# Gated linear attention and two MLPs: the first chunk's loads walked by groups of tokens

## The chip, the cores and the metric

The kernel runs on one core of one Trainium2 chip, in one launch. The metric is the time on the device in microseconds (us). The median of three runs before the change is 977.85 us (976.86 to 978.01).

A core has TensorE (matmuls; PE, with PEld for its weight loads), VectorE (DVE), ScalarE (ACT), GpSimd (POOL) and SyncE (SP), each with its own queue of instructions that it works through in order, and 16 DMA engines that carry what SyncE's and ScalarE's queues issue. SBUF is the on-chip memory of 128 partitions, PSUM the smaller one that TensorE writes.

## The reference

Four sequences (B) of 768 tokens (S) with 8 heads (H) of 48 features (D) go through a gated linear attention; its output, 3072 tokens of 384 features, goes through two MLPs of 2048 hidden units.

```
f = 1 / (1 + exp(-f_logit))
for t in range(S):
    state = f[:, :, t, :, None] * state + einsum('bhd,bhe->bhde', k[:, :, t], v[:, :, t])
    y[:, :, t] = einsum('bhd,bhde->bhe', q[:, :, t], state)
x = y with heads side by side, (B * S, H * D)
h = x @ w_in;   g = max(h, 0) + alpha * min(h, 0);  x = g @ w_out     # first MLP
h = x @ w_in2;  g = h - tanh(h);                    out = g @ w_out2  # second MLP
```

All is float32; the weights come as float64 and are decoded to float32 on the chip.

## The kernel before, in words

The 768 tokens are cut into 6 chunks of 128 (C). A step of the attention is one sequence and one chunk, 24 in all; steps 0 to 3 are the first chunk of the four sequences, and they are the ones with i < EARLY. A step has seven stages: f (transpose f_logit, make the gate, two scans up and down), k (transpose k and q, scale them to kd and qd), s0 and s1 (the scores sc = kd times qd, masked to a; kr and ks, kd turned back), y0 and y1 (the output y from a and v, split into x, the MLP's input), m (the new state from ks and v). A unit of the MLP is one chunk of all four sequences, 512 tokens, and one block of 128 hidden units: nine matmuls h (L451 to L453), the activation on ScalarE and VectorE, nine matmuls acc (L511). Its first needs x of all four steps of the first chunk and the first decoded block of weights.

Every load is issued by load_step (f, k, q and later v), load_v (v of the first chunk: va at L183, two vb at L185) or load_w (weights, L197 to L216), nearly all on SyncE's queue. For steps 0 to 3, each of f, k and q comes in two loads (L167), one for even heads and one for odd ones, 96 KB each. In such a load a partition holds four consecutive tokens (j) of one pair of heads, one row of 4 x 48 floats, 768 bytes; there are 32 groups of tokens (t) and four pairs (p), 128 partitions. From step 4 on, a load (L175) has one token in a partition, in rows of 192 bytes, and 192 KB. Of the 24 loads of L167, the three for odd heads of step 0 are issued by ScalarE, the other 21 by SyncE.

turned() puts features on the partitions. For steps 0 to 3 it makes eight matmuls (two halves of heads, four j) against the identity, so that a column of the PSUM tile is a partition of the loaded tile. The view that it returns orders these columns by pair, group and j again, and ScalarE (L266) and VectorE (L292, L294) read it through that view and write plain tiles. Nothing after that depends on how the load placed the rows.

The order of the stages and loads up to the first unit of the MLP is the list PROLOGUE, written by hand: loads of steps 0, 1, v of 0, step 2, the first weights, v of 1, step 3, v of 2, two more blocks of weights, with v of 3 and the loads of step 4 behind the stages of step 0. A planner that estimates times when the kernel is built then lays down each engine's order of instructions; on the chip each engine keeps that order. Behind the prologue, the list work places attention steps, loads and decoding of weights between the MLP's units by due times. Three buffers hold f, k and q by turns (NV), and three hold raw weights (NR), so later loads are issued as buffers come free.

Of the kernel before, what the change touches and what calls it, by code (L numbers as in the profile page):

```python
# [20 lines left out]
C = 128  # L21
NC = S // C
UT = B * C
NP = H // 2
# [46 lines left out]
def tile_main(tc, q, k, v, f_logit, w1_in, w1_out, alpha, w2_in, w2_out, out, flag):  # L71
    nc = tc.nc
    with ExitStack() as ctx:
# [37 lines left out]
        for b in range(2):  # L111
            t = const.tile([128, NP, 2, HW], F32, name=f"blocks{b}")
# [11 lines left out]
        def set_idle(t, nm):  # L124
            for a, b in ((4 * D, PAD), (PAD + 4 * D, H * HW)):
                nc.vector.memset(t[:, a:b], 30.0 if nm == "f" else 0.0)

        padded = {}
        for nm in ("f", "k", "q"):
            padded[nm] = []  # L130
            for j in range(NV):
                t = const.tile([128, H * HW], F32, name=f"{nm}{j}")
# [15 lines left out]
        def load_step(i):  # L148
            c, b = divmod(i, B)
            t0 = c * C  # L150
            s = {}
            for nm, a in (("f", f_logit), ("k", k), ("q", q), ("v", v)):
                if nm == "v" and c == 0:
                    continue
                if nm == "v":
                    t = s[nm] = ld.tile([128, H, D], F32, tag=nm, name=nm, bufs=NV)
                else:
                    if i == NV:
                        t = tp.tile([128, H * HW], F32, **{"f": dict(tag="g"), "k": dict(tag="g"), "q": dict(tag="neg", bufs=1)}[nm], name=nm)
                        set_idle(t, nm)  # L160
                    else:
                        t = padded[nm][i % NV]
                    if i < EARLY:

                        s[nm] = t[:, 0:2 * PAD].rearrange("p (h x) -> p h x", h=2)
                        for h in range(2):
                            (nc.scalar if i == 0 and h else nc.sync).dma_start(  # L167
                                out=s[nm][:, h, 0:4 * D],
                                in_=a[b, h::2, t0:t0 + C, :].rearrange("p (t j) d -> p t (j d)", j=4),
                            )  # L170
                        continue

                    s[nm] = t.rearrange("p (h x) -> p h x", h=H)
                    t = s[nm][:, :, 0:D]
                nc.sync.dma_start(out=t, in_=a[b, :, t0:t0 + C, :].rearrange("h t d -> t h d"))  # L175
            steps[i] = s
# [65 lines left out]
        def turned(i, nm, palloc):  # L242

            a = steps[i][nm]
            if i >= EARLY:
                t = palloc([128, NP, C], nm + "t")
                for p in range(NP):
                    nc.tensor.transpose(t[:, p], a[:, 2 * p:2 * p + 2, :].rearrange("t h d -> t (h d)"), ident)  # L248
                return t
            t = palloc([128, 4, 128], nm + "t")  # L250
            for j in range(4):
                for h in range(2):
                    nc.tensor.matmul(
                        out=t[HW * h:HW * h + HW, j], lhsT=a[:, h, j * D:j * D + HW], rhs=ident, start=True, stop=True
                    )
            return t.rearrange("p j (h t) -> p h t j", h=NP)

        def like(i, a):

# [2 lines left out]
        def attn_f(i, palloc):  # L262
            s = steps[i]
            gv = spread(gate[:, 0:NP * SEG])
            ft = turned(i, "f", palloc)
            nc.scalar.activation(out=like(i, gv), in_=ft, func=ACTF.Exp, scale=-1.0)  # L266
            if i < 2 * B:
                nc.scalar.activation(out=gv, in_=gv, func=ACTF.Identity, bias=ones[:, 0:1])  # L268
            else:
                nc.vector.tensor_scalar(out=gv, in0=gv, scalar1=1.0, scalar2=None, op0=ALU.add)  # L270
            up = at.tile([128, NP * SEG], F32, tag="up", name="up")
            nc.vector.tensor_tensor_scan(  # L272
                out=up, data0=gate[:, 0:NP * SEG], data1=reset, initial=0.0, op0=ALU.mult, op1=ALU.add
            )
            ends = up[:, C:NP * SEG:SEG]
            inv = carry[:, SEG:NP * SEG + 1:SEG]
            nc.vector.reciprocal(out=inv, in_=ends)
            nc.vector.tensor_tensor(out=worst, in0=worst, in1=ends, op=ALU.max)
            down = at.tile([128, NP * SEG + 1], F32, tag="down", name="down")
            nc.vector.tensor_tensor_scan(  # L280
                out=down[:, NP * SEG:0:-1], data0=gate[:, NP * SEG:0:-1], data1=carry[:, NP * SEG:0:-1],
                initial=0.0, op0=ALU.mult, op1=ALU.add,
            )
            ends = at.tile([128, NP], F32, tag="inv", name="inv", bufs=3)
            nc.vector.tensor_copy(out=ends, in_=inv)
            s.update(up=up, down=down, inv=ends)

        def attn_k(i, palloc):
            s = steps[i]
            kt, qt = turned(i, "k", palloc), turned(i, "q", palloc)  # L290
            kd = at.tile([128, NP, C], F32, tag="kd", name="kd")
            nc.vector.tensor_tensor(out=like(i, kd), in0=kt, in1=like(i, spread(s["up"])), op=ALU.mult)  # L292
            qd = at.tile([128, NP, C], F32, tag="qd", name="qd")
            nc.vector.tensor_tensor(  # L294
                out=like(i, qd), in0=qt, in1=like(i, spread(s["down"][:, 1:NP * SEG + 1])), op=ALU.mult
            )
            s.update(kd=kd, qd=qd, a=at.tile([128, 2, NP, C], F32, tag="a", name="a"))
# [282 lines left out]
        for ev in PROLOGUE:  # L580
            if ev[0] == "c":
                convert(0, ev[1])
            elif ev[0] == "w":
                load(0, ev[1])
            elif ev[0] == "l":
                load_step(ev[1])
            elif ev[0] == "v":
                load_v(ev[1])
            elif ev[0] == "a":
                nc.sync.dma_start(out=alpha_raw, in_=alpha.rearrange("(c p) -> c p", p=128))  # L590
            else:
                stage(*ev, wide)
# [10 lines left out]
        for i in range(B, NC * B):  # L603
            c, b = divmod(i, B)

            if c < 3:
                t0, order = (0.7, 24.7)[c - 1] + 1.85 * b, tight_order
            else:
                t0, order = (c - 1) * FC + 3 * b + (2.5 if c == 3 else 0.5), wide_order
            for st, t in order:  # L610
                if ("f", i) not in PROLOGUE or st != "f":
                    put(t0 + t, stage, st, i)
            if i >= B + NV:
                put(t0 - NV * (1.85 if c < 3 else 3) + 0.8, load_step, i)
        first = sum(ev[0] == "c" for ev in PROLOGUE)
        when = {2: 0, 3: 1.2, 4: 2.0, 5: 3.2, 6: 4.2, 7: 5.4}
        for n in range(2 * NG):
            t = when.get(n, 7.5 + 1.5 * (n - NG)) if n >= first else -0.3
# [10 lines left out]
        for n, (g, half) in enumerate(halves):  # L629
            t = max(last + 6 + 1.5 * n, last + 2 * g + 2 * half + 2.2)  # L630
# [173 lines left out]
```

## Time and profile before

| | us |
|---|---|
| median of three runs | 977.85 |
| the profiled execution | 977.85 |
| its span, first to last instruction | 975.8 |
| TensorE busy | 943.2 (97%) |
| VectorE busy | 560.9 (57%) |
| ScalarE busy | 408.4 (42%) |
| GpSimd busy | 9.6 (1%) |
| 62.68 MB by DMA, mean over the span | 64 GB/s |

The engines' shares are means over the span. A window gives the busy time of each engine in one stretch, TensorE's granted clock (1.00 is 2.4 GHz, 0.50 is 1.2), the mean share of time in which the 16 DMA engines had a packet under way (packets of several queues can overlap, so it can pass 1), and the bytes moved. A wait is put down to what ended last before the waiting instruction started.

### The profile page before, as it was taken

The page shows a single profiled execution, that of the slowest core. Times are in us where ns is not written, and L with a number is a line of the kernel's source. Part 1 is how long each engine was busy: PE and PEld are TensorE (multiplying, and loading weights), DVE is VectorE, ACT ScalarE, POOL GpSimd, SP SyncE. Part 2 cuts the span into 40 slices and gives each one's busy share as a digit, 9 for nine tenths or more (in the row PEclk, how much of TensorE's full clock was granted, in tenths as well). Part 3 has the DMA queues.
Part 4 walks back from the last instruction along what each step waited for, and adds up shares of the span by engine and source line. Part 5 has one row for each costly group of instructions (what it writes and reads, how often), then busy time and mean ns, then how long its engine had stood idle before and what let it go on. Part 6 is the DMA issues. An engine that isn't in the chain of part 4 may idle for free.

```text
span 975.8 us, 13398 instructions
## 1 busy us (share of the span) xinstructions
PE 943.2 (97%) x5299; PEld 779.7 (80%) x5299; DVE 560.9 (57%) x926; ACT 408.4 (42%) x721; POOL 9.6 (1%) x24
## 2 busy tenths in 40 slices
PE   5598999999999999999999999999999999999997
PEld 5577787888888887888888888888888888888896
DVE  5589998566655565456444899953343433433432
ACT  3265556444444443444344665532232332322222
POOL 2000000000000000000000000000000000000000
PEclk9789999999999999999999999999999999999999
DMA  4897845042421232112022336330030110200201
GB/s 103 149 190 162 148 107 116 9 110 44 82 50 33 49 85 47 25 36 62 8 67 65 122 105 194 98 65 0 1 66 1 22 44 0 33 1 1 33 1 35
DMA packets 154277, 62.68 MB, mean 64 GB/s; under 512 B 123856, under 2 KB 141664, under 8 KB 154208
## 3 DMA queue, kind: packets, MB, share of 16 engines
q1 hardware_dynamic: 153812, 61.47, 28.4%
q8 instruction: 43, 0.70, 0.3%
q10 hardware_dynamic: 396, 0.29, 0.1%
q14 instruction: 26, 0.21, 0.1%
HBM read 49.55 MB, written 10.22 MB: 61 GB/s over the span
## 4 chain that ended last, share of the span: by engine, by line
PE 90%; DMA 4%; DVE 3%; SPq 2%; issue 0%; ACT 0%; ACTq 0%; DVEq 0%
PE acc L511 40%; PE h L451 13%; PE h L452 13%; PE h L453 13%; PE sc L319 2%; PE y L366 2%; PE y L342 2%; DMA k<-in_k_dram 2%; PE kt L248 1%; DMA raw<-in_moe_w_in_dram 1%; PE m L401 1%; PE qt L248 1%; PE ft L248 1%; SPq L167 1%; PE kr L305 1%; DMA f<-in_f_logit_dram 1%
## 5 line engine op out<-in xcount | busy, mean ns | idle before, releaser
L451 PE MATMUL h<-x,wih 128*128 128x512 f32 x576 | 228.6, 397 | 2.4 <-DMA x<-x 2.4
L452 PE MATMUL h<-x,wih 128*128 128x512 f32 x576 | 225.0, 391 | 0.0
L453 PE MATMUL h<-x,wil 128*128 128x512 f32 x576 | 225.0, 391 | 0.0
L511 PE MATMUL acc<-gh,wol 128*128 128x512 f32 x528 | 206.8, 393 | 1.8 <-DVE wol L233 1.8
L511 PE MATMUL acc<-gl,woh 128*128 128x512 f32 x528 | 207.6, 393 | 0.0
L511 PE MATMUL acc<-gh,woh 128*128 128x512 f32 x528 | 201.4, 396 | 0.9 <-ACT woh L232 0.9
L472 ACT CAST gh<-g 128x512 fp32r<-128x512 f32 x192 | 119.2, 621 | 139.4 <-DVE g L464 73.6
L473 DVE TENSOR_TENSOR gl<-g,gh 128x512 fp32r<-128x512 f32 x192 | 132.1, 688 | 76.5 <-ACT gh L472 67.9
L464 DVE TENSOR_TENSOR g<-h,g 128x512 f32<-128x512 f32 x96 | 66.2, 689 | 146.0 <-ACT g L463 146.0
L459 DVE SCALAR_TENSOR_TENSOR g<-neg,alpha_neg,g 128x512 f32<-128x512 f32 x96 | 72.0, 750 | 123.1 <-ACT neg L458 123.0
L463 ACT ACTIVATE g<-h 128x512 f32<-128x512 f32 x96 | 57.5, 599 | 174.8 <-PE h L453 174.8
L451 PEld LDWEIGHTS h<-x,wih 128*128 128x128 f32 x576 | 108.2, 188 | 24.6 <-DMA x<-x 2.8
L453 PEld LDWEIGHTS h<-x,wil 128*128 128x128 f32 x576 | 108.1, 188 | 23.2 <-DVE dec L65 0.2
L452 PEld LDWEIGHTS h<-x,wih 128*128 128x128 f32 x576 | 108.3, 188 | 20.9
L511 PEld LDWEIGHTS acc<-gh,wol 128*128 128x128 f32 x528 | 99.3, 188 | 22.6 <-DVE wol L233 1.9
L511 PEld LDWEIGHTS acc<-gh,woh 128*128 128x128 f32 x528 | 99.1, 189 | 22.9 <-ACT woh L232 1.5
L511 PEld LDWEIGHTS acc<-gl,woh 128*128 128x128 f32 x528 | 99.6, 189 | 20.4 <-DVE gl L473 0.4
L457 ACT ACTIVATE g<-h 128x512 f32<-128x512 f32 x96 | 57.5, 598 | 130.5 <-PE h L453 129.6
L458 ACT ACTIVATE neg<-h 128x512 f32<-128x512 f32 x96 | 56.9, 593 | 0.0
L272 DVE TENSOR_TENSOR_SCAN up<-gate,reset 128x516 f32<-128x516 f32 x24 | 29.5, 1231 | 10.5 <-ACT gate L268 9.9
L319 PEld LDWEIGHTS sc<-qd,kd 48*128 48x128 f32 x384 | 26.5, 193 | 9.0 <-issue 4.6
L319 PE MATMUL sc<-qd,kd 48*128 48x128 f32 x384 | 31.4, 291 | 1.2 <-DVE qd L294 1.2
(99 smaller groups left out, 805.8 us busy)
## 6 DMA issues: line engine op xcount, KB each, us to landing
raw<-in_moe_w_out_dram SPq DMA_DIRECT2D x16, 768.0 KB
raw<-in_moe_w_in_dram SPq DMA_DIRECT2D x8, 768.0 KB
raw<-in_moe_w_in_dram SPq DMA_DIRECT2D x16, 288.0 KB
x1d<-o SPq DMA_DIRECT2D x24, 192.0 KB
x1raw<-x1d SPq DMA_DIRECT2D x6, 768.0 KB
f<-in_f_logit_dram SPq DMA_DIRECT2D x20, 192.0 KB
k<-in_k_dram SPq DMA_DIRECT2D x20, 192.0 KB
q<-in_q_dram SPq DMA_DIRECT2D x20, 192.0 KB
```

What stands on the lines that cost most here:

```text
L319: nc.tensor.matmul(out=sc[h][:, p], lhsT=s["kd"][r, p], rhs=s["qd"][r, p], start=True, stop=True)
L451: nc.tensor.matmul(out=h, lhsT=a, rhs=xh[:, r], start=(r == 0), stop=False)
L452: nc.tensor.matmul(out=h, lhsT=a, rhs=xl[:, r], start=False, stop=False)
L453: nc.tensor.matmul(out=h, lhsT=b, rhs=xh[:, r], start=False, stop=(r == 2))
L457: nc.scalar.activation(out=g, in_=h, func=ACTF.Relu)
L458: nc.scalar.activation(out=neg, in_=h, func=ACTF.Relu, scale=-1.0)
L459: nc.vector.scalar_tensor_tensor(out=g, in0=neg, scalar=alpha_neg[:, fc:fc + 1], in1=g, op0=ALU.mult, op1=ALU.add)
L463: nc.scalar.activation(out=g, in_=h, func=ACTF.Tanh)
L464: nc.vector.tensor_tensor(out=g, in0=h, in1=g, op=ALU.subtract)
L472: nc.scalar.copy(out=gh, in_=g)
L473: nc.vector.tensor_tensor(out=gl, in0=g, in1=gh.bitcast(F32), op=ALU.subtract)
L511: nc.tensor.matmul(out=t, lhsT=a, rhs=b, start=first and i == 0, stop=final and i == 2)
```

## The change

The access pattern of the 24 loads at L167 names the 32 groups of tokens first and the four pairs of heads second; before, it was the other way round. The rows, their 768 bytes and their count stay. So partition 4t + p holds group t of pair p, where it was 32p + t. The view at L256 takes that back: in a block of 128 columns the pair is now the inner part.

```
                             (nc.scalar if i == 0 and h else nc.sync).dma_start(
                                 out=s[nm][:, h, 0:4 * D],
-                                in_=a[b, h::2, t0:t0 + C, :].rearrange("p (t j) d -> p t (j d)", j=4),
+                                in_=a[b, h::2, t0:t0 + C, :].rearrange("p (t j) d -> t p (j d)", j=4),
                             )
...
-            return t.rearrange("p j (h t) -> p h t j", h=NP)
+            return t.rearrange("p j (t h) -> p h t j", h=NP)
```

## Rows read from the trace of the kernel before

**Rows 1.** The page's part 1: busy us of each engine, its share, instructions.

```profile
PE 943.2 (97%) x5299; PEld 779.7 (80%) x5299; DVE 560.9 (57%) x926; ACT 408.4 (42%) x721; POOL 9.6 (1%) x24
```

**Rows 2.** Windows by stage: length, busy us (instructions) by engine, TensorE's clock, DMA share, GB/s.

```profile
5.80:12.00 6.20, 5.10 (x50) 4.11 (x50) 2.79 (x5) 1.32 (x2) 0.00 (x0) 1.00 0.27 92
...
28.00:30.00 2.00, 0.66 (x2) 0.29 (x2) 0.57 (x2) 0.00 (x0) 0.00 (x0) 0.50 0.29 67
...
42.00:44.00 2.00, 2.00 (x46) 2.00 (x46) 0.62 (x3) 1.83 (x3) 1.20 (x2) 1.00 0.98 334
...
52.00:54.00 2.00, 1.61 (x10) 0.99 (x9) 1.97 (x5) 1.07 (x2) 0.83 (x2) 0.50 1.34 178
...
59.00:87.00 28.00, 25.38 (x187) 20.36 (x185) 27.96 (x49) 18.11 (x33) 0.00 (x0) 1.00 0.96 182
...
87.00:975.80 888.80, 879.99 (x4650) 726.63 (x4650) 501.54 (x800) 370.88 (x654) 0.00 (x0) 1.00 0.24 56
```

**Rows 3.** TensorE's waits, first 100 us: waiter, releaser, total us, times, longest.

```profile
PE ft L253 <- DMA f<-in_f_logit_dram: 8.4, 4, 5.8
...
PE y L354 <- DMA va<-in_v_dram: 5.4, 1, 5.4
...
PE m L401 <- DMA va<-in_v_dram: 2.1, 1, 2.1
```

**Rows 4.** Order of time on TensorE: start us, duration us, instruction [idle before, releaser].

```profile
5.78 1.98 PE L253 MATMUL ft<-ident,f 128*64 128x128 f32 x16 [5.78 <-DMA f<-in_f_logit_dram]
...
21.71 1.16 PE L319 MATMUL sc<-qd,kd 48*128 48x128 f32 x16
...
29.18 0.66 PE L354 MATMUL y<-a,va 128*64 128x128 f32 x2 [5.35 <-DMA va<-in_v_dram]
...
42.50 1.06 PE L253 MATMUL kt<-ident,k 128*64 128x128 f32 x16
...
44.91 0.82 PE L358 MATMUL y<-a,vb 128*64 128x128 f32 x12
...
48.01 0.52 PE L248 MATMUL ft<-ident,f 128*128 128x128 f32 x3 [2.27 <-DMA f<-in_f_logit_dram]
...
59.04 0.48 PE L451 MATMUL h<-x,wih 128*128 128x512 f32 x1
```

**Rows 5.** Order of time on SyncE's queue, its issues: start us, duration us.

```profile
0.82 0.75 SPq L167 DMA_DIRECT2D f<-in_f_logit_dram  x1
...
40.34 0.80 SPq L175 DMA_DIRECT2D f<-in_f_logit_dram  x1
```

**Rows 6.** SyncE's issues by line: ns min/median/max, first and last start us.

```profile
L167 SPq DMA_DIRECT2D q<-in_q_dram x7: 528/530/1664, 2.3 to 30.2; - x7
...
L183 SPq DMA_DIRECT2D va<-in_v_dram x4: 401/720/1873, 11.3 to 38.2; - x4
...
L185 SPq DMA_DIRECT2D vb<-in_v_dram x8: 546/995/1622, 12.3 to 39.4; - x8
...
L209 SPq DMA_DIRECT2D raw<-in_moe_w_in_dram x4: 434/436/444, 20.1 to 37.2; - x4
```

**Rows 7.** Order of time on GpSimd (first row) and VectorE.

```profile
23.61 1.23 POOL L325 TENSOR_SCALAR_AFFINE_SELECT a<-a 128x512 f32<-128x512 f32 x2 [5.16 <-ACT a L324]
...
38.24 0.69 DVE L292 TENSOR_TENSOR kd<-kt,up 128x512 f32<-128x512 f32 x1
...
47.38 0.96 DVE L65 SCALAR_TENSOR_TENSOR dec<-raw,dec 128x768 int32<-128x768 int32 x1
...
50.90 0.96 DVE L233 TENSOR_TENSOR wil<-dec,wih 128x768 fp32r<-128x768 f32 x1 [2.09 <-ACT wih L232]
...
51.77 1.23 DVE L272 TENSOR_TENSOR_SCAN up<-gate,reset 128x516 f32<-128x516 f32 x1
```

**Rows 8.** ScalarE's reads of PSUM by line: ns min/median/max.

```profile
L266 ACT ACTIVATE gate<-ft x6: 597/600/615, 7.8 to 59.4; 128x512 f32<-128x512 f32 x6
...
L307 ACT COPY ks<-kr x4: 586/586/604, 14.0 to 49.1; 128x512 f32<-128x512 f32 x4
```

## The prediction

> **What bounds the kernel now.** I read the engines' totals first [rows 1], then the windows by stage [rows 2], then TensorE's waits [rows 3], and last the order of time on TensorE, SyncE, VectorE and GpSimd [rows 4 to 7]. Over the whole span TensorE is busy 97%. After 87 us it is busy 879.99 of 888.80 us, and from 59 to 87 VectorE is busy 27.96 of 28.00 us while TensorE has 25.38 [rows 2]. So from 59.04 us, where the first matmul of the first layer starts [rows 4], the kernel runs at the pace of its engines. What can be saved is before that: the prologue, in which the four steps of the first chunk are computed. There TensorE's longest waits end with a DMA: 8.4 us for f in four waits (5.8 of it the start), 5.4 for va, 2.1 for va again [rows 3], 2.3 for the f of step 4 [rows 4].
>
> The view by windows says why these loads are late. From 5.8 to 12 us almost nothing but the loads of L167 is under way, and the DMA engines are busy 0.27 of 16, that is 4.3 engines, at 92 GB/s; from 28 to 30 us it is the same, 0.29 at 67 GB/s [rows 2]. From 42 to 44 us, with other loads, the same engines move 334 GB/s at a share of 0.98. So a load of L167 seems to run on four engines, as many as its outer dimension has entries.
>
> By the Trainium skill, "DMA: Bandwidth & Descriptors", section "Why a DMA increments its semaphore by 16 and not by 1", a DMA runs on the largest number of engines up to 16 that divides the slowest dimension of both its sides. By that rule it was gcd(4, 128) = 4 and becomes 16, and the trace's 0.27 agrees with the first half; the second half no run has shown yet.
>
> **The change, part by part.** It adds and removes no instruction. Each of the 24 loads of L167 (21 on SyncE's queue, 3 on ScalarE's) keeps its 128 rows of 768 bytes and its 96 KB; the order in which they are walked changes, and with it which partition holds which token and pair. That is undone by another view of the same PSUM tile at L256, read by three instructions a step.
>
> *The transposed read.* ACT at L266 and VectorE at L292 and L294 now step 1 over pairs and 4 over groups instead of 32 and 1; the innermost step stays 128 elements. ACT reads the present strided view in 600 ns and a plain 128x512 tile in 586 [rows 8]. So a stride of 128 costs at most 0.014 us; for 12 reads in four steps I take 0, between -0.2 and +0.2.
>
> *The transfer.* If 16 engines work on a load, 92 GB/s becomes at most four times that, 368; nearest row 334. The floor is no gain, 92. I take about 330, as the rows are neither shorter nor fewer. The 24 loads are 2.36 MB: 25.6 us of four engines' time at 92 GB/s, 7.1 at 334.
>
> *SyncE's queue.* It issues f of step 4 at 40.34 us [rows 5], after 43 issues: 21 of L167, 12 of v, 9 of weights, one of alpha. The queue starts at 0.82 us [rows 5]. At the shortest duration of each line (0.53 for L167, alpha taken the same; va 0.40 and vb 0.55; weights 0.43 [rows 6]), with 0.05 between two, f of step 4 goes out at 0.8 + 11.7 + 6.0 + 3.9 + 2.1 = 24.5 us. The other 15.8 us are issues held back by earlier loads that have not landed (L167 up to 1.66 us, against 0.53 [rows 6]). With quick landings they go. I take 0.53 for the new form too, between 0.43 (16 partitions or more, L209) and 1.66, the longest of its own line; the short values are those of a queue that isn't backed up.
>
> *The path through compute*, step by step:
> 1. First matmul: 5.78 us [rows 4]. Step 0's two f loads are 196 KB, 2.1 us at 92 GB/s and 0.6 at 334. I take 1.35 us of the 1.5, as the loads of k start in between.
> 2. Step 1: TensorE's 2.1 us for va go [rows 3], ft of step 1 no longer waits, and the scans of step 0 are the bound until step 1's run. The scores of step 1, at 21.71 [rows 4], come 2.6 to 4.0 us earlier; I take 3.3.
> 3. Its masks on GpSimd end at 23.61 + 1.23 = 24.84 [rows 7], so 21.5 in future. TensorE now waits until 29.18 for va [rows 4]; with va there, it starts y of step 1 at 21.5, 7.7 us earlier.
> 4. From there to kt of step 2, TensorE has y (2 x 0.82), kt (1.06), ft of step 3 (16 matmuls of the same shape, 1.06) and m (taken at 0.7, below the 1.06 of wider ones) [rows 4]: 4.5 us, to 26.0. Now kd of step 2 starts at 38.24 [rows 7]; the difference of 12.2 holds f's waits and the half clock of 0.50 [rows 2], which followed TensorE's idle time. Behind the waits VectorE's scans are late next (step 2's end 3.3 us earlier than now, about 25.3), so I count on 12.1.
> 5. The stretch from there to y of step 2 (44.91 + 0.82 = 45.73 [rows 4]) is compute and moves as it is. Then TensorE waits 2.3 us for f of step 4, 7.6 us after its issue. Issued at 24.5 it lands at about 32.1, and TensorE comes to it at 33.6: the wait goes, with 1.5 us to spare. But the weights' decoding on VectorE ends at 48.34 (47.38 + 0.96) and its scan at 51.77 [rows 7] must follow the weights' split (wil, 0.96 [rows 7], and ScalarE's cast before it, taken the same): not before 50.3. So 1.5 of the 2.3 count.
>
> The sum is 12.1 + 1.5 = 13.6 us if all of that holds, 12.9 with 2.6 in step 2, and 11.4 if the wait for f of step 4 also stays in another guise. I take 12.8: the first matmul of the layer then starts at 46.2 instead of 59.04. Behind it nothing is added: the stretch bound by VectorE and the one bound by TensorE move as a whole, since loads there are issued as buffers come free and move along (DMA share 0.96 from 59 to 87, so hardly more could be had).
>
> The profiled execution took 977.85 us (span 975.8 and 2.05 around it), which is the median of the runs. So 977.85 - 12.8 = 965.05.
>
> **Rivals.**
> *The issue eats part of it.* If an issue of L167 costs 0.9 us on 16 queues, f of step 4 goes out 21 x 0.37 = 7.8 us later, at 32.3, lands at 40 and binds: 8 us earlier than now, about 970. At 1.1 it is 974. The same comes out if small rows and weights together hold the queues back (shares of 0.98 from 42 us and 0.96 from 59 [rows 2]). For it: the longest issue of L167 took three times the shortest [rows 6]. Against it: L183 issues 768 rows in 0.40 at its best [rows 6].
> *More.* The clock is at 0.50 from 52 to 54 us again [rows 2], behind the wait for f of step 4. If it stays at 1.00 there, step 3's scores and y, some 6 us of TensorE's time, take 3 less, and with what is behind them 2 to 5: about 961. Against it: VectorE's chain runs beside them.
> *Nothing happens.* The DMA is split by its SBUF side or by rows, so four engines were the result of something else, and the order of rows changes nothing: 978. For it: only the share shows the four engines. Against it: 0.27 is too near to 4 of 16.
> *Slower.* The issuing itself pays for 16 queues and SyncE becomes the bound of the prologue: at 1.66 us an issue, 21 x 1.13 = 23.7 us more, f of step 4 goes out at 48.2, 8 us after 40.34: 986. It decides from (40.34 - 24.5)/21 + 0.53 = 1.28 us on; below that the change still wins.
>
> **How the numbers follow.** Forecast 965.0 (963 to 967.5): 0.57. Part eaten (968 to 975): 0.18. More (958 to 962.5): 0.11. Nothing: 0.07. Slower: 0.07. The range from 960 to 973.5 holds the first, most of the second and two thirds of the third, a little over 0.8. A measurement here tells about 0.2%, 2 us, from no change: faster 0.86, same 0.07, slower 0.07.
>
> **What would show it.** Right: from 5 to 10 us a DMA share far above 0.27 while only L167 loads; issues of L167 near 0.53; f of step 4 issued near 25 us; TensorE's waits for va and f under 2 us each after the start; the first L451 near 46; everything after it shifted alike. Wrong: a share still at 0.27; issues above 1.2 us; or a first L451 near 46 and an end that isn't earlier, which would mean that the stretch up to 87 us waits for loads I took to move along. Another order of TensorE's instructions, which a planner lays down at build time, would upset steps 2 to 5 in either direction.

## The result, and the profile after

The changed kernel takes 968.59 us (median of 4 runs, 965.62 to 969.34) beside 977.36 before: ratio 0.9899, 95% interval 0.9881 to 0.9917. It is faster by about 1%, 8.8 us; the forecast was 965.0 in a range of 960.0 to 973.5, so the direction and the range held and the forecast gain of 12.8 us was too large by some 45%. The profiled execution took 968.69 us, its span 966.7 instead of 975.8. The order of instructions on every engine is the one of before, so the two traces can be laid over each other mark by mark, a mark being the start of the same instruction in both.

First the transfer. Part 3 of the page of before (queue: packets, MB, share):

```profile
q1 hardware_dynamic: 153812, 61.47, 28.4%
q10 hardware_dynamic: 396, 0.29, 0.1%
```

and of after:

```profile
q1 hardware_dynamic: 154064, 61.47, 29.0%
q10 hardware_dynamic: 432, 0.30, 0.1%
```

SyncE's queue (q1) has 252 packets more, ScalarE's (q10) 36, with the same rows in the program: 12 for each of the 21 and of the 3 loads. ScalarE's queue carries these three loads and nothing else, so its packets can be counted whole: 396 is 3 x (128 + 4) and 432 is 3 x (128 + 16). The trace lists them as 384 packets of 768 bytes, the rows, both times, and packets of 4 bytes, 12 before and 48 after. That is what four engines becoming sixteen leaves behind, if each engine that takes part ends its share with a packet. By the Trainium skill, "DMA: Bandwidth & Descriptors", section "Why a DMA increments its semaphore by 16 and not by 1", each engine's last descriptor is that semaphore write; the counts agree.

Windows of after, with the columns of [rows 2]; the first and the last two answer to rows there:

```profile
5.80:12.00 6.20, 5.91 (x66) 5.49 (x64) 3.96 (x7) 2.78 (x5) 0.00 (x0) 1.00 0.61 137
...
24.00:26.00 2.00, 2.00 (x22) 2.00 (x20) 0.00 (x0) 0.00 (x0) 0.00 (x0) 0.50 0.76 144
28.00:30.00 2.00, 2.00 (x33) 1.78 (x28) 1.89 (x4) 1.72 (x4) 0.00 (x0) 1.00 0.83 192
...
59.00:87.00 28.00, 25.32 (x179) 20.41 (x180) 27.97 (x49) 16.21 (x30) 0.00 (x0) 1.00 0.88 165
```

From 5.8 to 12 us the share is 0.61 instead of 0.27, and TensorE works 5.91 of 6.20 us. VectorE is still full from 59 to 87. The clock is at 0.50 from 24 to 26 us. A stretch in which hardly anything but the loads of L167 is under way, from 4.0 to 7.5 us, before and then after:

```profile
4.00:7.50 3.50, 1.72 (x16) 1.75 (x17) 0.38 (x5) 0.54 (x1) 0.00 (x0) 1.00 0.28 94
```

```profile
4.00:7.50 3.50, 3.50 (x36) 3.50 (x34) 0.83 (x6) 1.40 (x3) 0.00 (x0) 1.00 0.58 168
```

So the share doubles, but the loads move 168 GB/s and not the forecast 330. SyncE issues one load of 96 KB every 0.64 us here, which is 154 GB/s by an estimate from these two numbers. So the pace of issues, and not the engines at a share of 0.58, seems to bound these loads now.

TensorE's waits in the first 100 us (as [rows 3]) and the order of time on it (as [rows 4]):

```profile
PE y L354 <- DVE worst L278: 5.3, 2, 3.4
PE ft L253 <- DMA f<-in_f_logit_dram: 3.9, 2, 3.6
...
PE ft L248 <- DMA f<-in_f_logit_dram: 1.3, 1, 1.3
```

```profile
3.65 1.97 PE L253 MATMUL ft<-ident,f 128*64 128x128 f32 x16 [3.65 <-DMA f<-in_f_logit_dram]
...
17.12 1.16 PE L319 MATMUL sc<-qd,kd 48*128 48x128 f32 x16
...
22.64 0.40 PE L354 MATMUL y<-a,va 128*64 128x128 f32 x2 [3.41 <-DVE worst L278]
...
37.58 0.52 PE L248 MATMUL ft<-ident,f 128*128 128x128 f32 x3 [1.32 <-DMA f<-in_f_logit_dram]
...
48.36 0.48 PE L451 MATMUL h<-x,wih 128*128 128x512 f32 x1
```

The matmul of y at 22.64 doesn't read worst; VectorE's instruction merely ended near that moment. The loads say what it was. The view of DMA issues, for the stretch from 16.4 to 16.8 us and then from 30.3 to 31.0 (KB, us from issue to landing):

```profile
va<-in_v_dram SPq DMA_DIRECT2D x1, 144.0 KB, 6.1
```

```profile
f<-in_f_logit_dram SPq DMA_DIRECT2D x1, 192.0 KB, 7.0
```

The issue of va of step 1, after and then before:

```profile
16.43 0.42 SPq L183 DMA_DIRECT2D va<-in_v_dram  x1
```

```profile
21.53 0.42 SPq L183 DMA_DIRECT2D va<-in_v_dram  x1
```

va of step 1 went out at 16.43 and landed at 22.5; f of step 4 went out at 30.41 and landed at 37.4. Both are what TensorE waited for, and both have blocks of weights ahead of them in the queue. SyncE's queue and L167's issues (as [rows 5, 6]), with the time to landing of L167's loads, and VectorE's marks (as [rows 7]):

```profile
30.41 0.92 SPq L175 DMA_DIRECT2D f<-in_f_logit_dram  x1
```

```profile
L167 SPq DMA_DIRECT2D q<-in_q_dram x7: 535/602/1607, 2.4 to 22.5; - x7
...
DMA to landing us min/median/max: 2.3/2.6/5.0
```

```profile
28.76 0.69 DVE L292 TENSOR_TENSOR kd<-kt,up 128x512 f32<-128x512 f32 x1
...
41.34 1.23 DVE L272 TENSOR_TENSOR_SCAN up<-gate,reset 128x516 f32<-128x516 f32 x1
```

So the first matmul of the layer comes 10.68 us earlier (59.04 to 48.36), and 9.1 reach the end of the span. In between the shift first grows, to 12.5 us from 92 to 100 us: the kernel before had a clock of 0.77 from 85 to 90 us, and the stretch that answers to it has 1.00. Then it falls, most of all at the first unit that needs x of the second chunk. The order of time on TensorE there, before:

```profile
119.68 0.47 PE L451 MATMUL h<-x,wih 128*128 128x512 f32 x1 [2.36 <-DMA x<-x]
...
120.92 0.39 PE L511 MATMUL acc<-gl,woh 128*128 128x512 f32 x1
```

and after:

```profile
108.33 0.52 PE L451 MATMUL h<-x,wih 128*128 128x512 f32 x1 [2.74 <-DMA x<-x]
...
110.36 0.63 PE L511 MATMUL acc<-gl,woh 128*128 128x512 f32 x1
```

After the same wait, 0.4 us longer, the matmuls take 0.63 us instead of 0.39 until 112 us; from 110 to 112 the granted clock is 0.50. The shift is 11.35 us at the first of these matmuls and 9.77 behind the last. From 124 us on it stays at 9.73 up to the last matmul, and the last 0.6 go behind that one, with the final stores.

### The profile page after: what moved, and what is told of

It is laid out like the page before. It is cut to its first block, busy times and chain, and to the rows that moved or that the text cites. A ratio compares the mean times of both kernels' runs of the same rounds, so it can differ in the third digit from the quotient of the medians.

```text
span 966.7 us, 13398 instructions
## 1 busy us (share of the span) xinstructions
PE 941.5 (97%) x5299; PEld 779.4 (81%) x5299; DVE 560.4 (58%) x926; ACT 408.3 (42%) x721; POOL 10.1 (1%) x24
## 4 chain that ended last, share of the span: by engine, by line
PE 90%; DVE 4%; DMA 3%; SPq 3%; issue 0%; ACT 0%; DVEq 0%
PE acc L511 40%; PE h L451 13%; PE h L452 13%; PE h L453 13%; PE y L366 2%; PE sc L319 2%; PE y L342 2%; SPq L167 1%; DMA k<-in_k_dram 1%; PE kt L248 1%; PE m L401 1%; PE ft L248 1%; PE qt L248 1%; PE kr L305 1%; DMA raw<-in_moe_w_in_dram 1%; SPq L175 1%
## 5 line engine op out<-in xcount | busy, mean ns | idle before, releaser
L451 PE MATMUL h<-x,wih 128*128 128x512 f32 x576 | 228.6, 397 | 2.7 <-DMA x<-x 2.7
L451 PEld LDWEIGHTS h<-x,wih 128*128 128x128 f32 x576 | 108.3, 188 | 25.0 <-DMA x<-x 3.1
```

Of the source, the lines that this page charges most:

```text
L451: nc.tensor.matmul(out=h, lhsT=a, rhs=xh[:, r], start=(r == 0), stop=False)
```

## Experiments

Each was timed beside the kernel before, on one chip. The edits are against the changed kernel, and some show parts of lines. In the first, only f walks the groups of tokens first:

```
-in_=a[b, h::2, t0:t0 + C, :].rearrange("p (t j) d -> t p (j d)", j=4),
+in_=a[b, h::2, t0:t0 + C, :].rearrange("p (t j) d -> t p (j d)" if nm == "f" else "p (t j) d -> p t (j d)", j=4),
...
-return t.rearrange("p j (t h) -> p h t j", h=NP)
+return t.rearrange("p j (t h) -> p h t j" if nm == "f" else "p j (h t) -> p h t j", h=NP)
```

> Only the loads of f walk groups of tokens first; k and q of steps 0 to 3 are loaded and read as before the change. Theory A (an L167 load ran on four engines and held back all that is queued behind it, whatever tensor it carries): 16 of 24 loads stay at four engines, 18.4 us of their time instead of 27.6, so about a third of the gain: first L451 near 55, about 974 us. Rival B (only the loads that TensorE is seen to wait for count, that is f and va): the gain stays whole, first L451 near 48.4, about 968.6 us.

Measured: 973.19 us, ratio 0.9962 (0.9946 to 0.9979). The first L451:

```profile
52.24 0.48 PE L451 MATMUL h<-x,wih 128*128 128x512 f32 x1
```

The gain is not whole, so rival B falls: slow loads of k and q cost too, although in the kernel before TensorE is seen to wait for them at L253 for 0.9 us only. How much of it f carries is not settled. By the ratios it is 0.0038 of 0.0101, theory A's third or somewhat more; by the mark at 52.24, nearly 3 us earlier than A said, it is 6.8 of 10.7 us, two thirds. The profiled execution was the fastest of the nine (969.91 to 977.19 us). The count of packets went up by 84 and 12, 12 for each of the seven and the one load of f.

The second makes the same choice by step, with `i < 2` in place of `nm == "f"`:

> The new order for steps 0 and 1 alone; steps 2 and 3 load as before. Theory A: first matmul at 3.65 and scores of step 1 near 17.1 as in the changed kernel, then the slow loads of f, k and q of steps 2 and 3 (12 x 1.15 us on four engines) hold va of step 1 and f of step 3 back by 3 to 5 us: first L451 at 51 to 53, about 971 to 973 us. Rival C (the gain is the early start, and what comes later is paced by SyncE's issues, which are as many): first L451 near 48.5, about 968.6 us.

Measured: 972.21 us, ratio 0.9944 (0.9926 to 0.9962), and

```profile
52.32 0.48 PE L451 MATMUL h<-x,wih 128*128 128x512 f32 x1
```

As theory A has it, and not C (the order of instructions is that of before, here and in f_only): the scores of step 1 come at 17.09 as in the changed kernel, then y of step 1 starts at 24.02 instead of 22.64 and kd of step 2 at 32.17 instead of 28.76. The loads of steps 2 and 3 carry about 4 of the 10.7 us.

The third asks where the missing part of the forecast is. It is the changed kernel with one entry of the list moved:

```
-("l", 2), ("w", 0), ("v", 1), ("l", 3), ("v", 2), ("w", 1), ("w", 2),
+("l", 2), ("v", 1), ("l", 3), ("v", 2), ("w", 0), ("w", 1), ("w", 2),
```

> The changed kernel with the first block of weights issued behind the loads of step 3 and v of step 2 instead of ahead of v of step 1. Theory D (the part of the forecast gain that is missing went to the 768 KB of weights queued ahead of va of step 1, which landed at 22.5 us): va lands near 18, y of step 1 starts when its masks are done, near 20.3 instead of 22.64, TensorE's idle time is short enough to keep its clock at 1.00, first L451 at 44.5 to 46.5 instead of 48.36, about 965 us. Rival C (SyncE's issues of 0.60 us set the pace; f of step 4 goes out near 30.4 either way): first L451 at 47.5 to 48.4, 967.5 to 968.6 us.

Measured: 967.16 us, ratio 0.9893 (0.9865 to 0.9921), no different from the changed kernel's 0.9899. The order of time on TensorE:

```profile
19.65 0.43 PE L354 MATMUL y<-a,va 128*64 128x128 f32 x2 [0.48 <-POOL a L325]
...
40.00 1.09 PE L248 MATMUL ft<-ident,f 128*128 128x128 f32 x4 [5.72 <-DMA f<-in_f_logit_dram]
```

Theory D is right on the first wait: va went out at 13.38 and landed 3.5 us after its issue, and y of step 1 starts at 19.65, 3 us earlier, with its masks as the releaser. kd of step 2 follows at 24.56 (28.76). But then all of it is lost in one wait: f of step 4 now lies behind three blocks of weights, goes out at 32.29 and takes 7.6 us. The first matmul of the layer is a little later than in the changed kernel:

```profile
49.33 0.48 PE L451 MATMUL h<-x,wih 128*128 128x512 f32 x1
```

The wait did not go, it moved one load down the queue; D's time for the whole was wrong by that. C's marks missed too, by 1 to 2 us, and the time lies between the two forecasts. The planner kept the changed kernel's order up to this wait, but put kr of step 3 ahead of it.

The fourth is the changed kernel with one load in place of two for each of f, k and q of steps 1 to 3:

```
+if i:
+    nc.sync.dma_start(
+        out=s[nm][:, :, 0:4 * D],
+        in_=a[b, :, t0:t0 + C, :].rearrange("(p h) (t j) d -> t p h (j d)", h=2, j=4),
+    )
+    continue
 for h in range(2):
```

> The changed kernel with one load instead of two for each of f, k and q of steps 1 to 3 (256 rows of 768 bytes in one issue): nine issues fewer. Rival C (issues set the pace): 9 x 0.65 = 5.9 us earlier on SyncE's queue, f of step 4 goes out near 24.5, first L451 at 43 to 46, 963 to 966 us. Theory D alone: the weights and va of step 1 go out 3.9 us earlier and land near 18.6, y of step 1 near 20.3, first L451 at 45 to 46.5, about 966 us. If a merged issue costs as much as two (1.2 us) nothing changes: 968.6 us.

Measured: 963.41 us, ratio 0.9859 (0.9831 to 0.9887). SyncE's issues at L167, and the first matmul of the layer (six lines further down in this kernel):

```profile
L167 SPq DMA_DIRECT2D q<-in_q_dram x3: 612/612/1370, 5.1 to 16.3; - x3
```

```profile
43.46 0.48 PE L457 MATMUL h<-x,wih 128*128 128x512 f32 x1
```

An issue of 256 rows costs 0.61 us, no more than one of 128. f of step 4 goes out at 24.68 instead of 30.41, as C said, and the layer starts 4.9 us earlier. So the number of SyncE's issues does set when these loads go out. That it alone gives the 4.9 us is not shown, because the planner laid down another order with fewer loads: the scores and y of step 1 now stand behind ft of step 3, and y behind kt and qt of step 2 too, where the changed kernel has both, or their first matmuls, ahead of these.

```profile
19.77 1.09 PE L259 MATMUL ft<-ident,f 128*64 128x128 f32 x16 [1.61 <-DMA f<-in_f_logit_dram]
20.79 1.16 PE L325 MATMUL sc<-qd,kd 48*128 48x128 f32 x16
...
24.15 0.97 PE L360 MATMUL y<-a,va 128*64 128x128 f32 x11
```

So TensorE no longer stands still for va of step 1, which landed at 18.92, 7.2 us after its issue. And its clock was at 1.00 all the way from 14 to 48 us, where the changed kernel has two stretches at 0.50, from 24 to 26 and from 44 to 47. C fell as the explanation of the gain in the second experiment; for what was left of it, it holds on SyncE's queue.

The last three were timed together, on another chip. w_late has the edit of w0_late and also moves the second and third block of weights behind the loads of step 4 (shown against w0_late):

```
-("l", 3), ("v", 2), ("w", 0), ("w", 1), ("w", 2),
+("l", 3), ("v", 2), ("w", 0),
...
-("m", 1), ("l", 4), ("k", 2),
+("m", 1), ("l", 4), ("w", 1), ("w", 2), ("k", 2),
```

> As w0_late, and besides the second and third block of weights (1.5 MB) issued behind the loads of step 4 instead of ahead of them. Theory D (what TensorE waits for lies behind weights in the queues): f of step 4, which landed at 39.87 behind them, lands at 28 to 31, TensorE no longer waits for it, first L451 at 43 to 45 instead of 49.33, about 962 to 964 us. Rival E (the engines' own chain of scans, masks and decoding is the bound by then): first L451 at 47 to 49 and about 967 us. Rival F: the first L451 comes early but its second block of weights comes late, the units of the MLP wait and the end stays near 967 us.

Measured: 965.10 us, ratio 0.9868 (0.9837 to 0.9898).

```profile
33.30 0.41 PE L248 MATMUL ft<-ident,f 128*128 128x128 f32 x2 [0.99 <-DVE qd L294]
...
46.87 0.77 PE L451 MATMUL h<-x,wih 128*128 128x512 f32 x1
```

f of step 4 goes out at 26.54 instead of 32.29 and lands at 33.16 instead of 39.87, later than D's 28 to 31. TensorE's first matmul on it follows 0.14 us behind the landing, as in the other runs, so the 0.99 us before it still end with f, although they are put down to VectorE, which ended at 33.20. The wait of 5.72 us is down to that, so the weights ahead of f were the cause of most of it. But of these 6.7 us only 2.5 reach the first L451, at 46.87, just ahead of E's 47 to 49 and well behind D's 43 to 45. That the engines' own chain is the bound by then fits this, but isn't shown: the planner also moved two of the matmuls on f ahead of y of step 2, and the clock was at 0.50 from 42 to 48 us. In time it is between D and E; F, a late second block, would have shown as a first L451 as early as D's, and didn't.

merged_w has both edits, the merged loads and these weights:

> The merged loads and the weights moved as in w_late. Theory D: f of step 4 lands at 24 to 28 instead of 32.0, TensorE's 2.2 us for it go, first L451 at 40.5 to 42 instead of 43.46, 959 to 962 us. Rival E: the chain through VectorE is the bound, first L451 stays at 43 to 44, about 963 us. Rival F: the second block of weights comes late, 964 us or more.

Measured: 960.96 us, ratio 0.9820 (0.9789 to 0.9850), with

```profile
41.68 0.48 PE L457 MATMUL h<-x,wih 128*128 128x512 f32 x1
```

That is D's forecast, and the fastest kernel here, faster than both kernels of the case. Its order of instructions is that of merged, so this pair shows the move of the weights by itself: f of step 4 lands at 27.65 instead of 32.02, TensorE's wait of 2.2 us for it is gone, and the first matmul of the layer is 1.8 us earlier. In time the intervals of the two overlap, so what that adds in the end is not settled.

> The changed kernel as it is, timed beside the two above on one chip. First L451 at 48.4 again in any theory. Theory G (1.6 us of the gain are lost because TensorE's clock falls to 0.50 after its wait for x near 106 us): where the profiled execution shows the clock at 1.00 from 108 to 114 us, its time is 966 to 967; where it shows 0.50 there, 968.5 to 969. Rival: the time does not follow the clock there.

Measured: 968.07 us, ratio 0.9906 (0.9877 to 0.9934), and the profiled execution of 968.04 us again has the clock at 0.50 from 110 to 112. Theory G had 968.5 to 969 for that, so by the time it missed by 0.5, and no profile of this kernel with the clock at 1.00 there came to compare: this run settles nothing. The first L451 came at 48.99 and not at 48.4. What shows G is the pair of traces above, matmuls of 0.63 instead of 0.39 us and a shift smaller by 1.6, and a second pair: f_only and early01 start the layer within 0.1 us of each other, with one order of instructions, and differ in the clock behind the wait for x of the second chunk. From 112 to 116 us, f_only and then early01:

```profile
112.00:116.00 4.00, 4.00 (x19) 3.28 (x19) 3.96 (x8) 0.00 (x0) 0.00 (x0) 1.00 0.60 107
```

```profile
112.00:116.00 4.00, 3.65 (x9) 3.00 (x10) 4.00 (x9) 0.00 (x0) 0.00 (x0) 0.57 0.82 141
```

At its first matmul behind the wait early01 is 0.61 us behind, at 117 us it is 2.21, and from 120 us to the last matmul 2.23. So the half clock costs about 1.6 us there, and none of it comes back.

## Why the prediction was right, and where its size was off

The cause was as forecast: the loads of L167 ran on four engines, and the change spreads them. The reads of PSUM through the new view cost nothing (ScalarE's at L266 has a median of 602 ns, 600 before; VectorE's at L292 682, 686 before). The steps, one by one:

- *The transfer*: 330 GB/s taken, 168 measured while hardly anything else was under way. The pace of issues seems to bound it, which the forecast had only as a term of SyncE's queue.
- *First matmul*: 2.13 us earlier, 1.35 expected. The first loads land faster than I allowed.
- *Scores of step 1*: 4.59 earlier, 3.3 expected.
- *y of step 1*: 6.54 earlier, 7.7 expected. Here the prediction said that va would be there. It wasn't. By the terms of its sum va goes out at about 13.7 us (alpha and 15 loads of L167 at 0.53, three of v, four of weights, 0.05 between two); it went out at 16.43. And I had no term for a load issued behind 768 KB of weights, which landed 6.1 us after its issue. In w0_late, without the weights ahead, it went out at 13.38 and landed 3.5 us later, with no wait for it. The trace of before had a hint: va went out there at 21.53, and TensorE's wait for it ended 7.7 us later, at 29.18.
- *kd of step 2*: 9.48 earlier, 12.1 expected. The 4.5 us of TensorE's work took 6.1 (22.64 to 28.76): behind the wait of 3.4 us the clock was at 0.50 from 24 to 26 us. In w0_late, with the same order in this stretch and the clock at 1.00 from 19 to 25 us, it took 4.91 (19.65 to 24.56). This is the largest part that was mis-sized: 1.1 us of wait, 1.2 of clock and 0.4 of work.
- *f of step 4*: expected out at 24.5 and landed at 32.1, in fact 30.41 and 37.4. An issue on 16 engines takes 0.60 us, not 0.53, which is 1.5 us in 21; va and vb cost 0.7 us more than their shortest durations of before; and 3.7 us were issues still held back (one of q took 1.61, one of weights 1.10) and longer pauses between issues. Of TensorE's wait there 1.3 us stayed. That is the first rival, "the issue eats part of it", at a smaller price: it was given 0.9 us an issue.
- *Behind 59 us*: I took the rest to move as a whole. Up to 100 us it did, and gained 1.6 us more behind 85 us, where the kernel before had a lower clock; then the wait for x of the second chunk came with a lower clock behind it and took back 1.6. The forecast had neither, and that they nearly cancel is luck.

The sum failed in the term of steps 3 and 4 and in the queue's arithmetic, which used the shortest duration of each line for all of its issues and had no term for what lies ahead in the queues. The rival on the slower side (1.66 us an issue) was far off, and the rival "nothing happens" is refuted by the counts of packets. The rival "more" needed the clock to stay up ahead of the layer, and in the changed kernel it didn't:

```profile
44.00:47.00 3.00, 3.00 (x27) 2.63 (x26) 1.85 (x6) 0.51 (x2) 0.00 (x0) 0.50 1.28 173
```

## What to carry to other kernels

Look at the DMA share in a stretch in which one kind of load runs alone: here a share near 4 of 16 came from the access pattern, and walking the longer dimension first lifted it for 0.07 us more an issue. Then ask when each load lands by what is ahead of it in the queue, not by when it is issued, and move bulk loads that are needed late behind small ones that are needed soon; the wait may only move to the next load, so follow it until an engine is what ends it. When transfers are quick, the count of issues is the next price: fewer, larger loads. And when an order is planned at build time, look at it before a difference is put down to an edit of the loads.

## What the runs showed of the hardware that I had not expected

An issue of 256 rows on SyncE's queue took 0.61 us and one of 128 rows 0.60, while the same 128 rows on four engines took 0.53 (medians; for the last those of k and q). And the clock behind the wait for x of the second chunk: over nine profiles it fell to 0.50 behind that wait in six (waits of 2.4 to 2.8 us) and stayed at 1.00 in three (before 2.4, f_only 2.5, merged 2.2). The length of the wait alone does not decide; what else does is open.
